# An explicit order of 1786 pieces in place of a list schedule, in a fused attention and gated MLP kernel

## The chip, the cores and the metric

The kernel runs on one core of one Trainium2 chip. The metric is the device time of one execution in microseconds (us), as a median of several runs. The core has five engines with a queue of instructions each: TensorE (PE, matrix products; PEld is its weight load), VectorE (DVE), ScalarE (ACT), GpSimd (POOL) and SyncE (SP), which here only issues DMAs. Each engine takes its own instructions strictly in the order in which the program lists them, and waits on semaphores for what other engines and DMAs have to deliver first.

## The reference

```python
def _attn_ref(q, k, v, n_sink, window):          # B, H, S, D = 4, 8, 768, 64
    scores = scale * np.matmul(q, k.transpose(0, 1, 3, 2))
    keep = is_sink | in_window                    # 4 sink keys, and the last 128 keys
    scores = np.where(keep, scores, -1000000000.0)
    a = np.exp(scores - np.max(scores, axis=-1, keepdims=True))
    a = a / (np.sum(a, axis=-1, keepdims=True) + 1e-09)
    return np.matmul(a, v)

def _moe_ref(x, w_in, w_spatial, b_spatial, w_out):   # x: 4, 768, 512
    h = np.maximum(x @ w_in, 0.0)                     # 512 -> 1024
    u, v = h[..., :512], h[..., 512:]
    v_n = (v - mu) / np.sqrt(var + 1e-06)             # over the last axis
    v_s = np.einsum('ts,bsd->btd', w_spatial, v_n) + b_spatial[None, :, None]
    return (u * v_s) @ w_out
```

The attention's output, its heads put side by side, is the x of the second function.

## The kernel before

There are 4 batches b, each of 6 tiles t of 128 positions. A tile is worked in two halves of four heads; the half number i = 2 * (6 b + t) + half runs from 0 to 47. Nearly all products run in f16, with each f32 operand split into a high and a low half (`high`, `low`, `low_scaled`, L577 to L612), so that one product is three passes: high by high, high by low, low by high (`three`, L619).

The work is cut into 1786 pieces, each one closure for one engine, registered by `plan.add` with a name, the engines that may take it, a price, and what it reads and writes. The pieces by name:

- Weights: `w_in 0` (the half of w_in that makes u), `w_in 1` (the half that makes v) and `w_out` come as f64 words; each of 12 chunks is loaded (L616), decoded (ACT L641, DVE L643 and L646, POOL L649) and split (`... split`: high L583 to L592, low L607 on DVE or the pair L609 and L610 on POOL). `w_sp` is f32, six chunks of 128x768, loaded and split likewise.
- Attention, for each half i: `score` (PE L844, eight products into four PSUM banks "sc"), four `mask` (DVE L849), four `exp` (ACT L854), `p high` and `p low` (a 128x1024 copy and a subtraction), two DMA transposes `turn high` and `turn low` issued by SP (L921), then `av` (PE L963 to L971). After both halves of a tile: `divide` (DVE L977 to L979) and a turn of x into xT, by PE transposes in the first tiles (`x cross`, L1013 and L1029) and by DMA later (`x turn`, L1000). Tiles 0 and 1 of batch 0 do their attention in f32 with PE transposes (`p cross`, L884).
- MLP: `ps_v` (PE, L622 and L1055) and `v relu`, `v stats`, `v root`, `v norm`, `vn high`, `vn low` for each tile; `ps_u` and `u relu` for each pair of tiles c0 and quarter d; `ps_s` (PE, all six vn tiles of a batch by w_sp), `gate`, `times`, `g high`, `g low` for each (b, c0, d); `ps_o` (PE L1164), `o copy` (L1175, L1177) and `o store` for each output tile. `ps_v`, `ps_u`, `ps_s`, `ps_o` and the PE transposes share two PSUM banks.
- Range checks (`v check`, `w check`, `check`, L704 to L763): v of batch 0 and the weights are read again, and one flag is formed: three DVE steps, a PE transpose (L751), three more DVE steps (L754 to L756). Every engine loads the flag at the end (L1229), and a general path follows if it is set.

`Plan.order` (L281) is a list scheduler: it plays the pieces through with their prices, with ring sizes and with ranks from the table `WHEN`, takes at each step the piece that can start first on an engine that may take it, and so fixes the engine of each piece and the order of each engine's queue. Where its model leaves PE idle ahead of a piece, `warm` (L519) puts fill products ahead of it, 128x248 products on the identity (L526) that nobody reads; the trace shows 56 of them. `check_ranges()` is called last, at L1214, and the planner leaves the transposing of the flag to the end of PE's queue. The order is emitted piece by piece under a manual schedule (L1215 to L1218).

Of the kernel before, what the change touches and what calls it, by code (L numbers as in the profile page):

```python
# [58 lines left out]
def general_path(tc, wf, qk, v, w_in, w_sp, b_sp, w_out, out):  # L59

    nc = tc.nc
    with (
# [46 lines left out]
        for b in range(B):  # L109
# [112 lines left out]
WHEN = {  # L222
    "p cross": (-7645.87,), "x cross": (-946.982,), "x copy": (-7684.67,), "pt copy": (-1378.19,),
    "qk load": (-4637.88, 832.975), "k sink": (-5707.62, -5463.63), "k copy": (-1001.25, -1158.33),
    "score": (-8509.54, -5574.54), "mask": (-5653, -3159.62), "exp": (-3128.31, 26.9811),
    "p high": (-5712.46, -4860.97), "turn high": (1126.36, -4889.17), "sink high": (-4766.44, -660.912),
    "sink low": (-1161.58, -1729.28), "p low": (-4294.7, -1248.23), "turn low": (-7503.49, -1155.83),
    "av": (-7132.32, -4355.89), "divide": (-4638.21, -4891.2), "x high": (-4655.36, -1108.11),
    "x low": (-9179.28, 688.315), "x turn": (1169.15, -1217.83), "v load": (-5315.45, 1085.95),
    "v sum": (-6868.55, -1941.04), "v check": (807.025,), "w check": (-1093.24,), "check": (-1155.04,),  # L230
    "v sink": (-7755.39, -946.192), "v high": (-4580.5, -1033.28), "v low": (-5057.21, -4564.35),
    "ps_v": (-5726.43, -1424.26), "v relu": (-4061.2, -1875.91), "v stats": (-1602.66, -987.246),
    "v root": (-9057.1, -4615.84), "v norm": (-8861.23, 1176.72), "vn high": (-4790.37, -1623.78),
    "vn low": (1788.02, -4613.58), "ps_u": (698.347, -1389.6), "u relu": (-3425.42, -1209.25),
    "ps_s": (-1766.1, -3895.91), "gate": (-7760.54, -4767.95), "times": (-1391.34, -1703.34),
    "g high": (703.784, 1087.49), "g low": (-4790.01, 220.472), "ps_o": (-5395.94, -5449.72),
    "o copy": (-2357.65, 704.671), "o store": (-4810.26, -7722.48), "w_in 1 load": (1768.73, -2689.71),
    "w_in 1": (-5162.73, -533.079), "w_in 1 split": (-1242.8, -4597.23), "w_in 0 load": (-8938.98, 1073.29),
    "w_in 0": (-999.782, -5625.87), "w_in 0 split": (1151.13, -883.018), "w_sp load": (-905.754, -1162.84),
    "w_sp split": (-879.562, -1410.66), "w_out load": (-1070.21, -6959.45), "w_out": (-2070.07, -1261.38),  # L240
    "w_out split": (745.032, -1267.5), "q 0": (-7481.31,), "w 0": (-5528.28,), "w 1": (-4758.02,), "v 0": (-5236.43,),
    "w 2": (-1040.43,), "v 1": (-1241.46,), "w 3": (-873.723,), "v 2": (-8862.13,), "q 1": (-7703.79,),
}
GAP = {"o": 1.0228e-13, "pace": 0.09559, "pace 0": 0.65293, "s": 1.9808e-08, "u": 2.0431e-06, "w_in 0": 0.00052094, "w_in 1": 1.469e-13, "w_out": 12.175, "w_sp": 62.955}
CROSSED = 2
TURNED = 6
PACED = ("qk load", "k copy", "score", "mask", "exp", "p high", "p cross", "pt copy", "turn high", "sink high", "sink low",
         "p low", "turn low", "av", "divide", "x copy", "x high", "x low", "x turn", "x cross", "v load", "v sum", "v sink", "v high", "v low", "ps_v", "v relu",
         "v stats", "v root", "v norm", "vn high", "vn low")
IN_TURN = ("u", "vn", "q", "pexp", "pT", "p16", "xT", "x16", "av", "sc", "vraw")  # L250
STRICT = ("p16",)
LATENCY = {"PE": 0.25, "d": 0.15, "a": 0.18, "p": 0.12}
# [11 lines left out]
QUEUED = 3.0  # L264
TURNS_AHEAD = 3.66
WARM_FROM, WARM_SHARE, WARM_ONE = 4.0, 0.5, 0.108


class Plan:

    def __init__(self, rings, ring_of, warm):
        self.pieces, self.rings, self.ring_of, self.warm = [], rings, ring_of, warm

    def add(self, name, step, b, engines, time, f, reads=(), writes=(), dma=None, shared=False):

        if name in PACED:
            step = 2 * NT * b + (step - 2 * NT * b) * GAP["pace" if b else "pace 0"]
        rank = step + WHEN[name][min(b, len(WHEN[name]) - 1)]
        self.pieces.append((rank, len(self.pieces), engines, time, f, tuple(reads), tuple(writes), dma, shared))

    def order(self):  # L281
        ps = sorted(self.pieces, key=lambda x: x[:2])
        n = len(ps)
        place = {x[1]: i for i, x in enumerate(ps)}
        before, seen, users, takes = [set() for _ in ps], {}, {}, {}
        for _, k, _, _, _, reads, writes, _, _ in self.pieces:
            i = place[k]
            for key, wr in [(k, False) for k in reads] + [(k, True) for k in writes]:
                base, part = key[:2], key[2:]
                if not wr and base not in seen:  # L290
                    raise RuntimeError(f"plan: {key} is read before it is written")
                for j, part2, wr2 in seen.setdefault(base, []):
                    if (wr or wr2) and (part == part2 or not part or not part2):
                        before[i].add(j)
                seen[base].append((i, part, wr))
                users.setdefault(base, set()).add(i)
        after = [[] for _ in ps]
        for i, b in enumerate(before):
            b.discard(i)
            for j in b:  # L300
                after[j].append(i)
        turn = {}
        for i in range(n):
            for key in ps[i][5] + ps[i][6]:
                base = key[:2]
                ring = self.ring_of.get(base[0])
                if ring and base not in takes:
                    takes[base] = ring
                    turn.setdefault(ring, []).append(base)
        held = {r: [] for r in self.rings}  # L310
        slots = {r: [None] * n for r, n in self.rings.items()}
        left = {b: len(u) for b, u in users.items()}
        until = {b: 0.0 for b in users}
        taken = set()
        missing = [len(b) for b in before]
        ready = [0.0] * n
        free = {"PE": 0.0, "d": 0.0, "a": 0.0, "p": 0.0, "SP": 0.0, "port": 0.0}
        moved = 3.07
        idle, pe = {}, WARM_FROM
        open_ = [i for i in range(n) if not missing[i]]  # L320
        out, room_at = [], {}

        def room(i):

            t, new = 0.0, {}
            for base in dict.fromkeys(key[:2] for key in ps[i][5] + ps[i][6]):
                ring = takes.get(base)
                if ring is None or base in taken:
                    continue
                k = len(held[ring]) + new.get(ring, 0)  # L330
# [3 lines left out]
                if ring in STRICT:  # L334
                    old = slots[ring][k % len(slots[ring])]
                    if old and left[old]:
                        return None
# [938 lines left out]
```

## Time and profile before

| what | value |
| --- | --- |
| median of 3 runs | 434.6 us (433.96 to 435.53) |
| the profiled execution's own time | 430.26 us |
| its span, first to last instruction | 428.5 us |
| mean granted TensorE clock | 0.978 |
| busy PE, DVE, ACT, POOL | 400.3, 336.9, 228.2, 172.0 us |

Busy time of PE is from the first to the last moment at which a product is on its way, so a stretch can show PE busy though products follow one another at half their possible pace; how far PE got is read from its pieces, at the time that each takes when nothing holds it up. A granted clock of 1.00 is the 2.4 GHz level of TensorE; 0.50 would be the 1.2 GHz level, and values between are a mix of both within a stretch.

### The profile page before, as it was taken

The numbers are of one execution on the slowest core, as the hardware profiler recorded it, in microseconds if no ns is written. First come the engines' busy times: TensorE is split into PE (matmuls) and PEld (weight loads), VectorE is DVE, ScalarE is ACT, GpSimd is POOL, SyncE is SP. The second block draws the span as 40 slices with busy tenths as digits, with TensorE's granted clock in tenths as the row PEclk, the third lists the DMA queues.
The fourth block names the chain that finished last, engine by engine and source line by source line (L and its number), as shares of the span: only waits on it lengthen the run. The fifth ranks groups of instructions, "written<-read, shape, count | busy, mean of one in ns | idle before, by whom it ended". The sixth has DMA issues, their size and how long they took to land.

```text
span 428.5 us, 9641 instructions
## 1 busy us (share of the span) xinstructions
PE 400.3 (93%) x3561; PEld 283.3 (66%) x3561; DVE 336.9 (79%) x943; ACT 228.2 (53%) x527; POOL 172.0 (40%) x207
## 2 busy tenths in 40 slices
PE   5598987989999999999999999999999899999992
PEld 4376555657777856756876658576786586586771
DVE  3999999799999999888986973489899884553441
ACT  2799595679777876577774541266532211211100
POOL 4757967675878943656421220052133220100000
PEclk9699998989999999999999999999999999999997
DMA  6999898799999898999997802496998761001011
GB/s 222 306 337 236 231 204 172 180 189 229 230 247 193 179 221 150 253 218 194 205 229 209 121 29 59 86 140 119 142 204 243 243 148 50 24 26 50 0 50 57
DMA packets 139655, 70.98 MB, mean 166 GB/s; under 512 B 112464, under 2 KB 125776, under 8 KB 139600
## 3 DMA queue, kind: packets, MB, share of 16 engines
q1 hardware_dynamic: 139456, 70.28, 73.3%
q8 instruction: 30, 0.49, 0.5%
q14 instruction: 25, 0.20, 0.1%
q10 hardware_dynamic: 144, 0.00, 0.0%
HBM read 36.71 MB, written 6.29 MB: 100 GB/s over the span
## 4 chain that ended last, share of the span: by engine, by line
PE 63%; DVE 23%; DMA 5%; issue 4%; ACT 2%; POOL 1%; SPq 0%; DVEq 0%; ACTq 0%; POOLq 0%
PE ps_s L622 17%; PE ps_o L1164 14%; PE ps_v L622 11%; PE ps_u L622 10%; PE sc L844 6%; DVE pexp L849 5%; DVE p L599 4%; DVE vring L607 2%; DMA dec<-w_in 2%; DVE g L1149 2%; PE av L969 2%; DVE w L646 2%; DVE w L643 1%; PE av L971 1%; PE av L970 1%
## 5 line engine op out<-in xcount | busy, mean ns | idle before, releaser
L622 PE MATMUL ps_s<-wsp,vn 128*128 128x256 f16 x864 | 100.1, 273 | 1.3 <-ACT ob L1175 1.3
L854 ACT ACTIVATE pexp<-pexp,nm 128x260 f32<-128x260 f32 (+1 forms) x192 | 83.8, 484 | 25.8 <-DVE nm L849 25.2
L622 PEld LDWEIGHTS <-vn 128*128 128x128 f16 x864 | 83.4, 98 | 14.4 <-issue 3.1
L622 PE MATMUL ps_u<-xT,win 128*128 128x256 f16 x576 | 69.8, 275 | 3.2 <-DVE xT L1019 2.7
L599 POOL TENSOR_TENSOR p<-pexp,p 128x16 f16<-128x16 f32 (+2 forms) x47 | 47.5, 1015 | 44.1 <-ACT p L583 30.9
L1164 PE MATMUL ps_o<-wout,g 128*128 128x512 f16 x288 | 64.8, 379 | 0.3 <-ACT u L1115 0.3
L622 PEld LDWEIGHTS <-win 128*128 128x128 f16 x576 | 55.5, 99 | 14.3 <-issue 6.1
L844 PE MATMUL sc<-kring,q 64*128 64x260 f32 (+1 forms) x384 | 58.4, 405 | 6.3 <-DMA q<-qk_t 4.1
L622 PE MATMUL ps_v<-win,xT 128*128 128x512 f16 x264 | 62.1, 387 | 0.0
L844 PEld LDWEIGHTS sc<-kring,q 64*128 64x128 f32 x384 | 36.9, 195 | 22.2 <-DVE nm L849 6.8
L1081 POOL TENSOR_TENSOR rs<-rs,mhalf 128x1 f32<-128x1 f32 x24 | 17.4, 726 | 80.8 <-DVE rs L1078 80.0
L1137 DVE SCALAR_TENSOR_TENSOR g<-ps_s,b_bc 128x256 f32<-128x256 f32 x48 | 20.2, 420 | 37.6 <-PE ps_s L622 37.2
L1164 PEld LDWEIGHTS <-g 128*128 128x128 f16 x288 | 27.5, 98 | 32.8 <-issue 2.2
L622 PEld LDWEIGHTS <-xT 128*128 128x128 f16 x264 | 25.7, 99 | 29.1 <-issue 3.4
L1115 ACT ACTIVATE u<-ps_u 128x256 f32<-128x256 f32 x48 | 18.1, 377 | 45.8 <-PE ps_u L622 45.6
L969 PE MATMUL av<-vring,pT 128*128 128x65 f16 x328 | 34.0, 193 | 2.0 <-DVE x L979 2.0
L599 DVE TENSOR_TENSOR p<-pexp,p 128x1024 f16<-128x1024 f32 (+2 forms) x29 | 35.0, 1209 | 0.6 <-ACT p L583 0.6
L1175 ACT ACTIVATE ob<-ps_o 128x512 f32<-128x512 f32 (+1 forms) x24 | 13.9, 579 | 39.3 <-PE ps_o L1164 35.0
L971 PE MATMUL av<-vring,pT 128*128 128x65 f16 x328 | 33.9, 193 | 0.0
L970 PE MATMUL av<-vring,pT 128*128 128x65 f16 x328 | 33.9, 193 | 0.0
L969 PEld LDWEIGHTS <-pT 128*128 128x128 f16 x328 | 30.2, 97 | 4.4 <-issue 3.0
L970 PEld LDWEIGHTS <-pT 128*128 128x128 f16 x328 | 30.1, 97 | 0.7
(131 smaller groups left out, 661.8 us busy)
## 6 DMA issues: line engine op xcount, KB each, us to landing
vraw<-v_s SPq DMA_DIRECT2D x30, 260.0 KB, 4.1
out<-ob SPq DMA_DIRECT2D x24, 256.0 KB, 2.1
kring<-qk_t SPq DMA_DIRECT2D x23, 256.0 KB, 4.4
q<-qk_t SPq DMA_DIRECT2D x23, 256.0 KB, 3.9
dec<-w_in SPq DMA_DIRECT2D x8, 512.0 KB, 7.2
pexp<-w_in SPq DMA_DIRECT2D x8, 512.0 KB, 4.8
wsp<-w_sp_t SPq DMA_DIRECT2D x6, 384.0 KB, 4.8
dec<-w_out SPq DMA_DIRECT2D x4, 512.0 KB, 4.3
```

The lines of the kernel that those rows point to most:

```text
L599: eng[e].tensor_tensor(out=o, in0=x, in1=hi, op=ALU.subtract)
L622: nc.tensor.matmul(o, a, m, start=(i == 0), stop=(i == n - 1))
L844: nc.tensor.matmul(view(h + q)[0], tl("q", (b, t))[rows, hp, :], keys, start=True, stop=True)
L849: nc.vector.tensor_tensor_reduce(out=po, in0=o, in1=mask, scale=-0.125, scalar=3.0e38, op0=ALU.add, op1=ALU.min, accum_out=nm()[:, q:q + 1])
L854: nc.scalar.activation(po, po, AF.Exp, bias=nm()[:, q:q + 1], scale=-1.0)
L969: nc.tensor.matmul(o[:, h], ph, vh, start=(t < 2 and j == 0), stop=False)
L970: nc.tensor.matmul(o[:, h], ph, vl, start=False, stop=False)
L971: nc.tensor.matmul(o[:, h], pl, vh, start=False, stop=(j == nb - 1 and (t < 2 or h == HH - 1)))
L1081: nc.gpsimd.tensor_tensor(out=vals["rs", i], in0=vals["rs", i], in1=mhalf, op=ALU.pow)
L1115: plan.add("u relu", r, b, "a", 0.365, lambda e: nc.scalar.activation(tl("u", (b, c0))[:, d, :], tl("ps_u", i)[:, :TC], AF.Relu, scale=G_U ...
L1137: nc.vector.scalar_tensor_tensor(out=g(), in0=tl("ps_s", i)[:, :TC], scalar=G_S, in1=b_bc[:, t0:t0 + TC], op0=ALU.mult, op1=ALU.add)
L1164: nc.tensor.matmul(o, lead, wout[:, w, d, :], start=(d == 0 and j == 0), stop=(d == KC - 1 and j == 2))
```

## The change

The tables `WHEN`, `GAP`, `PACED` and others, the costs for the planner and the list scheduler go. In their place stands `ORDER`, 1786 words, one for each piece, in the order in which they are emitted. A word is the number of the piece (in the order of the `plan.add` calls), a letter for its engine (P is PE, S is SP, a ACT, d DVE, p POOL) and, for PE, the number of fill products ahead of it.

```diff
+ORDER = """
+107S 117S 108a 109a 116S 122P7 123d 129d 118S 35S 127d 120p 213p 262p 36a 37d 38d 121p 159p 125d 126a 110d 39p
+28S 29a 119S 134P2 137d 135d 139d 30d 138a 130a 128a 136a 140a 49S 51d 124a 131P11 158S 157S 50a 31d 32p 52d 141d
...
+1630a 1745P 1746d 1747d 1748a 1749d 1756P 1757d 1758d 1759d 1760d 1702P 1703d 1750P 1751a 1753P 1754a 1755S 1761P
+1762d 1726S 1752S 1763d 1764d 1765d 1766P 1767d 1768d 1769d 1770d 1771P 1772d 1773d 1774p 1775d 1776P 1781P 1777P
+1779d 1782P 1778a 1780S 1784d 1783a 1785S
+"""
...
     def order(self):
+        listed, left = [], set(range(len(self.pieces)))
+        for word in ORDER.split():
+            n = next(j for j, x in enumerate(word) if not x.isdigit())
+            i, e, fill = int(word[:n]), word[n], int(word[n + 1:] or 0)
+            engines, f, writes = self.pieces[i]
+            e = {"P": "PE", "S": "SP"}.get(e, e)
+            assert e == engines or e in engines
+            left.remove(i)
+            listed.append((self.warm(writes[0], fill, f) if fill else f, e))
+        assert not left
+        return listed
...
-        def low_scaled(name, step, b, n, views, scale, reads, writes, engines="dp"):
+        def low_scaled(name, step, b, n, views, scale, reads, writes):
 
             def f(e):
                 o, x, hi = views()
-                if e == "d":
-                    nc.vector.scalar_tensor_tensor(out=o, in0=x, scalar=scale, in1=hi, op0=ALU.mult, op1=ALU.subtract)
-                else:
-                    nc.gpsimd.tensor_scalar(x, x, scale, 1.0, op0=ALU.mult, op1=ALU.mult)
-                    nc.gpsimd.tensor_tensor(out=o, in0=x, in1=hi, op=ALU.subtract)
+                nc.vector.scalar_tensor_tensor(out=o, in0=x, scalar=scale, in1=hi, op0=ALU.mult, op1=ALU.subtract)
...
-                             [("ps_o", i)], [("ob", i, j)])
+                             [("ps_o", i), ("flag", 0)], [("ob", i, j)])
...
+            if b == B - 1:
+                check_ranges()
             for c0 in range(S // TC):
...
-        check_ranges()
         order = plan.order()
```

No instruction of the computation is added. Read off the list, piece by piece, against the order that the trace of before shows, this is what differs:

- The engine of a piece. `p high`: 38 on ACT and 6 on DVE (before 20 and 24). `p low`: 18 on DVE, 26 on POOL (26 and 18). `vn low`: 9 on DVE, 15 on POOL (17 and 7). `times`: 24 and 24 (34 on DVE, 14 on POOL). `x high`: 9 on ACT, 8 on DVE, 6 on POOL (20, 2, 1). Low halves of w_in, w_sp and w_out: all on DVE (11 of them were pairs on POOL); their high halves on ACT and DVE alone.
- Fill products: 25 (7, 2 and 11 ahead of the first three PE pieces, then 3, 1 and 1), before 56 (48 ahead of the first score, then 7 and 1).
- The first loads on SP: a 97.5 KB tile of v_sink, then the first halves of q and k (128 KB each), then the second half of k, then w_in. Before: four 512 KB chunks of w_in, v, both v_sink tiles, then k and q.
- The place of the attention halves in PE's queue: the first score is first in both; half 18 stands behind 79 us of PE work (before 71), half 22 behind 124 us (96), half 30 behind 162 (137), half 40 behind 226 (183), half 46 behind 261 (254). Between a score of the halves 22 to 45 and its own `av` lie 15.4 us of other PE work on average, 10.8 at the least (before 29.3 and 13.8).
- The first `ps_s` stands behind 66.1 us of PE work, before behind 71.8.
- The PE transpose of the flag stands ahead of `ps_o` (3, 1, 0), and the three DVE steps that form the flag ahead of the gates of the last c0; the last DVE pieces are the two halves of `o copy`.

## Rows read from the trace of the kernel before

**Rows 1.** Busy time in four stretches: start:end, length, then as headed (x: instructions).
```profile
core 0: us, PE busy (x) PEld busy (x) DVE busy (x) ACT busy (x) POOL busy (x), PEclk, DMA share, GB/s
0.00:15.18 15.18, 6.53 (x48) 5.30 (x49) 7.72 (x15) 7.04 (x14) 8.26 (x27) 0.96 0.79 246
15.18:50.00 34.82, 31.61 (x234) 23.18 (x235) 34.62 (x98) 28.76 (x66) 25.74 (x28) 0.92 1.07 290
0.00:107.72 107.72, 89.45 (x760) 63.64 (x761) 96.09 (x260) 79.01 (x188) 71.71 (x92) 0.94 0.94 232
152.28:420.66 268.38, 266.72 (x2342) 186.11 (x2341) 195.90 (x565) 114.59 (x263) 63.00 (x73) 1.00 0.63 134
```
**Rows 2.** Chain that ended last, in time: start us, us, what.
```profile
155.03 1.08 PE sc L844 x8
168.76 3.93 PE ps_s L622 x36
183.03 2.59 PE ps_v L622 x12
200.68 1.31 PE ps_u L622 x12
```
**Rows 3.** Timeline of the start: start us, us, engine, line, operation, tiles [idle before <-releaser].
```profile
1.18 2.91 SPq L616 DMA_DIRECT2D dec<-w_in  x4
...
6.72 1.54 SPq L814 DMA_DIRECT2D kring<-qk_t  x2
...
9.17 1.58 SPq L816 DMA_DIRECT2D q<-qk_t  x2
...
15.18 1.23 PE L844 MATMUL sc<-kring,q 64*128 64x128 f32 x8 [4.08 <-DMA q<-qk_t]
```
**Rows 4.** DMA issues: tiles, queue, count, KB each, median us to landing.
```profile
pT<-p SPq DMA_TRANSPOSE x88, 3.6
...
kring<-qk_t SPq DMA_DIRECT2D x2, 128.0 KB, 5.5
q<-qk_t SPq DMA_DIRECT2D x2, 128.0 KB, 4.8
```
**Rows 5.** Groups, 0 to 107.72 us, DVE then POOL: count | busy us, mean ns.
```profile
L599 DVE TENSOR_TENSOR p<-pexp,p 128x1024 f16<-128x1024 f32 x6 | 10.2, 1700 | 0.0
L607 DVE SCALAR_TENSOR_TENSOR vring<-vraw,vring 128x512 f16<-128x512 f32 x9 | 9.6, 1071 | 0.0
L607 DVE SCALAR_TENSOR_TENSOR win<-w,win 128x512 f16<-128x512 f32 x6 | 8.0, 1379 | 0.0
L588 DVE CAST p<-pexp 128x1024 f16<-128x1024 f32 x6 | 5.0, 832 | 0.1
L607 DVE SCALAR_TENSOR_TENSOR wsp<-wsp 128x768 f16<-128x768 f32 x1 | 1.8, 1751 | 0.0
...
L610 POOL TENSOR_TENSOR wsp<-wsp 128x768 f16<-128x768 f32 x5 | 9.5, 1894 | 0.4
L609 POOL TENSOR_SCALAR wsp<-wsp 128x768 f32<-128x768 f32 x5 | 5.9, 1174 | 0.1
```
**Rows 6.** One line's instructions on DVE, whole span: count, ns least/median/most.
```profile
L607 DVE SCALAR_TENSOR_TENSOR vring<-vraw,vring x23: 680/695/2120, 13.6 to 286.1; 128x512 f16<-128x512 f32 x23
```
**Rows 7.** Timeline, halves 4 and 27: score on PE, both transposes on SP.
```profile
26.68 1.15 PE L844 MATMUL sc<-kring,q 64*128 64x260 f32 x8
...
32.67 4.37 SPq L921 DMA_TRANSPOSE pT<-p  x2
...
159.57 1.15 PE L844 MATMUL sc<-kring,q 64*128 64x260 f32 x8
...
173.15 2.66 SPq L921 DMA_TRANSPOSE pT<-p  x2
```
**Rows 8.** Timeline of DVE at the end.
```profile
421.16 0.42 DVE L1177 TENSOR_SCALAR ob<-ps_o 128x256 f32<-128x256 f32 x1 [0.22 <-ACT ob L1175]
...
421.98 0.14 DVE L756 CAST flagi<-checks 1x1 int32<-1x1 f32 x1
```

More of the change, by code (lines that the diff above doesn't have):

```diff
@@ L220 @@
          "xT": 2, "g": 2, "g2": 6, "w32": 8, "xT32": 1}
[L222 to L243, printed above, removed]
@@ L269, with __init__ @@
+1762d 1726S 1752S 1763d 1764d 1765d 1766P 1767d 1768d 1769d 1770d 1771P 1772d 1773d 1774p 1775d 1776P 1781P 1777P
+1779d 1782P 1778a 1780S 1784d 1783a 1785S
+"""
 class Plan:
-    def __init__(self, rings, ring_of, warm):
-        self.pieces, self.rings, self.ring_of, self.warm = [], rings, ring_of, warm
+    def __init__(self, warm):
+        self.pieces, self.warm = [], warm
     def add(self, name, step, b, engines, time, f, reads=(), writes=(), dma=None, shared=False):
[L276 to L279, printed above, removed]
+        self.pieces.append((engines, f, tuple(writes)))
@@ L281, in order @@
     def order(self):
[L282 to L330, printed above, removed]
-                if ring in IN_TURN and turn[ring][k] != base:
-                    return None
-                j = new[ring] = new.get(ring, 0) + 1
[L334 to L337, printed above, removed]
-                    t = max(t, until[old] if old else 0.0)
-                    continue
-                ends = sorted(until[b] if b else 0.0 for b in slots[ring] if b is None or not left[b])
-                if len(ends) < j:
-                    return None
-                t = max(t, ends[j - 1])
-            return t
@@ L408, in order @@
-        if len(out) != n:
-            raise RuntimeError("plan: pieces left")
-        self.end = max(until.values())
-        final = []
-        for k, (t, i, f, e) in enumerate(out):
-            if i in idle:
-                _, since, key = idle[i]
-                count = int((t - max(since, room_at.get(i, 0.0))) * WARM_SHARE / WARM_ONE)
-                if count > 0 and self.takes_bank(key):
-                    f = self.warm(key, count, f)
-            final.append((t, k, f, e))
-        return [(f, e) for _, _, f, e in sorted(final, key=lambda x: x[:2])]
@@ L556, in fast_path @@
         }
-        rings = dict(RINGS, ksink=1, **BANKS)
-        rings.update({f"{kind}{j}": 1 for kind in ("kslot", "vslot", "vsink") for j in range(4)})
-        plan = Plan(rings, dict({k: r for k, (r, _) in makers.items()}, **{r: r for r in rings}), warm)
+        plan = Plan(warm)
         tiles = {}
@@ L624, in early @@
         def early(x, name, step, b):
-            return (x, 0) if b == 0 and x in WHEN else (name, step)
+            return (name, step)
         vals = {}
@@ L662, in w_in_half @@
                            lambda c=c, i=i, hi=hi: (win[:, 1, c, f0:f0 + 512], tl("w32", i), hi()), SW_IN,
-                           [("w32", i), ("win", half, (0, c))], [("win", half, (1, c))], "d" if half else "dp")
+                           [("w32", i), ("win", half, (0, c))], [("win", half, (1, c))])
         def w_spatial():
-            gap = GAP["w_sp"]
+            gap = 1
             for c in range(NT):
@@ L680, in w_out_all @@
         def w_out_all():
-            gap = GAP["w_out"]
+            gap = 1
             for c in range(KC):
@@ L859, in scores @@
                 queries, keys = [("q", (0, 0), hf)], [(f"kslot{kslot(0, 0)}", (0, 0), (0, hf))]
-            plan.add("score", i, b, "PE", 1.05 if t else 0.75, product, queries + keys, banks)
+            plan.add("score", i, b, "PE", 1.08 if t else 0.75, product, queries + keys, banks)
             for q in range(n):
```

186 lines of the change are left out of this document (93 added, 93 removed).

## The prediction

> **What bounds the kernel now.** Begin with busy time by stretch [rows 1]. From 152 us to 420.66 PE is busy 266.7 of 268.4 us at a clock of 1.00: there TensorE is the bound, and only less waiting on it can help. In the first 107.72 us, up to the first `ps_s`, DVE is busy 96.1 us, and it has nothing to do before 7.86: of 99.9 us it works 96.1. There VectorE is the bound. PE looks busy for 89.4 of these 107.7 us, but that is elapsed pipeline time. What PE has got through is counted in pieces at their unhindered time [rows 2]: 1.08 us for a score, 3.93 / 2 = 1.97 for a `ps_s`, 2.59 for a `ps_v`, 1.31 for a `ps_u`. Ahead of the first `ps_s` stand 19 scores (18.8 us, the two halves without earlier keys being shorter), 12 `ps_u` (15.7), 6 `ps_v` (17.4, the two in f32 taken at 3.5), 15 `av` (13.5) and 12 crosses (6.3): 71.8 us of PE work, done in 107.72. So PE loses 107.7 - 71.8 = 35.9 us ahead of that piece.
>
> The rest is accounted in the same way. All PE pieces sum to 378 us; PE's last product ends at 420.66 [rows 1], and 428.5 - 420.66 = 7.8 us of tail follow. Lost later is then 428.5 - 378 - 35.9 - 7.8 = 6.8 us. The forecast replaces three of these terms: 35.9, 6.8 and 7.8. The 378 stays, as the change adds and removes no product but fill products.
>
> The start is in the timeline [rows 3]: SP issues w_in from 1.18, k only at 6.72 and q at 9.17, and the first score waits for q until 15.18. So 15.2 of the 35.9 us are the wait for q, and 20.7 are lost behind DVE.
>
> **The change: the order of the start.** Ahead of q and k now stands one v_sink tile. At some 0.75 us an issue (1.54 and 1.58 us for two [rows 3]) q and the first k half are issued between about 2.0 and 3.5 us. They land 4.8 and 5.5 us after issue at the median [rows 4], so the first score starts between 6.6 and 8.9 us; I take 7.9, 7.3 earlier than now. What pays is w_in: it moves behind four issues on SP, 3 us, and its decoding starts that much later. DVE has the sink's split and the first masks to fill this with.
>
> **The order of DVE's work, and low halves on DVE.** I counted the pieces that stand ahead of the first `ps_s` on DVE in both orders. At mean durations the old order has 88.5 us there. Removed: 5 `p high` at 0.83, 3 `p low` at 1.70, 5 masks at 0.35, 4 sink splits at 0.5, and some 5.3 us of smaller ones, 18.3 us in all. Added: 5 low halves of w_sp at 1.75, 2 of w_in at 1.38, 4 high halves of w_in at about 0.5, 2 decodes at 0.7 and four pieces of 0.2 to 0.8, 17.1 us [rows 5]. So DVE's own list is level, about 87.3 us: the change moves as much onto DVE as it takes off it. ACT has 73 us ahead of that point before and 65 after, so it is not late.
>
> What changes is POOL. It loses five w_sp pairs at 1.17 + 1.89 us (15.4 us), two w_in pairs (3.8) and six high halves (6.0), and gains two `p low` at about 2.1 and an x high: 68 us become 44. This matters to DVE because its durations stretch when POOL works: the same 128x512 subtraction takes 0.68 us at the least, 2.12 at the most [rows 6], and 1.07 on average in the first 107.7 us; the win form of the same size averages 1.38 [rows 5]. That excess is 9 x 0.39 = 3.5 us for v and 6 x 0.69 = 4.1 us for win; with the decodes, the `p low` and the rest of DVE's forms against their own least I make it 17 us in the stretch. A third of POOL's work goes, so I take a third of the excess off DVE, 6 us; the ends are 0, if what stays on POOL meets DVE as often, and 14, if the w_sp pairs did most of the harm. 87.3 - 6 = 81.3 us. By the Trainium skill, "SBUF — State Buffer", section "SBUF: two separate sides", GpSimd and a VectorE instruction with two SBUF inputs take turns on one shared port pair, each holding it for its whole instruction; the spread of 0.68 to 2.12 us fits that. By it the added two-input pieces on DVE would be exposed too, and the gain would be 4 to 5 us instead of 6.
>
> DVE's idle time while it is the bound: 3.8 us now; I take 4, and 7 if the later w_in leaves a hole (the share of the DMA engines is 1.07 between 15 and 50 us [rows 1], but DVE idles only 0.2 us there, so DMA is not what it waits for).
>
> DVE is then through with what the first `ps_s` needs at 7.9 + 81.3 + 4 = 93.2 us. That piece now stands behind 66.1 us of PE work (three scores, two `av` and one `ps_u` fewer), so PE loses 93.2 - 66.1 = 27.1 us ahead of it, where it lost 35.9. Ends: 6.6 + 73.3 + 4 - 66.1 = 17.8; and 8.9 + 87.3 + 1.5 + 7 - 66.1 = 38.6, where the 1.5 is for w_sp pieces that POOL stretches on DVE.
>
> **The order of the attention.** Halves 22 to 45 now have 15.4 us of PE work between a score and its `av`, 10.8 at the least, where 29.3 stood before. In between lie masks, exps, the two copies and two turns. For half 4, which was wanted early, the second turn was issued 9.2 us after the score's end (27.83 to 37.04); for half 27, 15.1 us (160.72 to 175.81) [rows 7]; a landing comes 3.6 us after its issue [rows 4], some 2.2 after the end of a pair of issues. So the chain takes 11.3 us when hurried and about 17.5 unhurried. PE executes its queue in order: behind an `av` that waits, everything waits. I take it that queues with little in them give the hurried time, and leave the later loss at 6 us; ends 3 and 13. Fewer `p high` on DVE and later deadlines for v and w checks speak for that.
>
> **The flag.** The last copy on DVE ends at 421.58, and the flag's last step at 422.12 [rows 8]. With the flag formed earlier the end hangs on the copies: -0.5 us, tail 7.3 (ends 7.0 and 7.8). The PE transpose of the flag, 0.2 us, now stands ahead of three groups of `ps_o`; PE would wait there if the re-read weights were not summed by then, but ACT is busy only 115 of the last 268 us [rows 1] and has room. The three DVE steps now delay the last gates by some 0.5 us, which the `ps_o` queued on PE covers; without that cover they cost that 0.5.
>
> **The sum.** 378 + 27.1 + 6 + 7.3 = 418.4 us of span, against 428.5. The profiled execution took 430.26, 1.8 above its span, and stands 4.3 under the median of the runs, so 418.4 + 1.8 + 4.3 = 424.5. Low: 378 + 17.8 + 3 + 7.3 = 406.1, or 412.2. High, with the first loss at its worst: 378 + 38.6 + 6 + 7.8 = 430.4, or 436.5.
>
> **Rivals.** *Nothing gained: DVE stays the bound, undisturbed by POOL's relief.* With no excess removed and 7 us of idle behind the later w_in, 7.9 + 87.3 + 7 - 66.1 = 36.1 lost, and 378 + 36.1 + 6.9 + 7.5 = 428.5: 434.6, the old time. For it: DVE's list is level and q is not what DVE waits for. Against: the earlier first score, and the row's spread of 0.68 to 2.12.
>
> *Slower: the attention chain no longer fits.* If the chain from score to `av` keeps its 17.5 us where the list leaves 15.4, PE waits in proportion over the 131 us of work between scores 22 and 45: 131 x (17.5 / 15.4 - 1) = 17.9 us, 442.4. It outweighs the gain of 10.1 from 15.4 x (1 + 10.1 / 131) = 16.6 us on. For it: half 27. Against: half 4 [rows 7], and that DVE's and ACT's queues drain faster in that stretch.
>
> *The clock.* Before the first score stand 48 fill products, of 6.5 us, and the granted clock is 0.96 up to 15.18 and 0.92 up to 50 [rows 1]. With 7 there and PE waiting on DVE between its pieces, PE could stay at the 1.2 GHz level until about 50 us; it has some 24 us of work by then, which would take twice as long, and the first 42 us would not hold them: about 7 us, 431.5. Against: the clock stayed at 0.92 with half of PE's time lost. The Trainium skill, "TensorE: Matmul & The Clock Gate", section "What's actually happening", has the throttled level as the default that activity releases; no row here shows PE at that level for long.
>
> *It doesn't do what it says.* Hardly possible: an order is executed as listed. What could differ is only a wait that a new order adds.
>
> **How the numbers follow.** Forecast 0.68; nothing gained 0.12; chain 0.11; clock 0.09. A measurement tells 0.3%, 1.3 us, from no change. Faster: the forecast's 0.68, the clock's 0.09 and 0.03 of "nothing gained"; same: 0.06 of it; slower: its last 0.03 and the chain's 0.11. The range, 412 to 437, takes in the ends of the first loss, the clock and nothing gained; left out are the chain (0.11) and some 0.08 of the forecast beyond its ends.
>
> **What would show it.** In the new profile: a first score at 7 to 9 us; the first `ps_s` near 93; POOL busy less by a third up to there, and the 128x512 low halves on DVE nearer to 0.9 than to 1.07 and 1.38; no wait of PE above 2 us on a turn after 120 us; the last copy, not the flag, as DVE's last step. Wrong if the first `ps_s` starts after 103, if waits of `av` for DMA sum to more than 6 us, or if the granted clock up to 50 us is near 0.5.

## The result, and the profile after

The changed kernel takes 411.98 us (411.48 to 412.96, four runs) against 435.06 us for the kernel before: 0.947 of it, with an interval of 0.944 to 0.950. The profiled execution took 412.96 us, its span is 411.2. That is 23 us faster where 10 were forecast, and just below the range of 412 to 437.

First the stretches, by the columns of [rows 1]: to where PE's loss stops growing (58.73), to the first `ps_s` (85.09), and from there to 403.50.

```profile
0.00:58.73 58.73, 49.04 (x398) 34.10 (x399) 49.46 (x167) 46.39 (x101) 31.88 (x56) 0.97 0.95 252
0.00:85.09 85.09, 75.31 (x657) 52.78 (x658) 73.36 (x237) 68.83 (x150) 44.78 (x70) 0.98 0.99 251
85.09:403.50 318.41, 314.40 (x2872) 222.68 (x2870) 231.56 (x695) 161.83 (x371) 116.42 (x141) 1.00 0.72 154
```

The first `ps_s` starts at 85.09 with 66.1 us of PE work ahead of it: 19.0 us are lost up to there, 36 before. POOL is busy 44.8 us up to there, 71.7 before. PE's pieces show where the loss arises: 6.2 us at the first score, 12.2 at the first `p cross`, 18.2 at 58.7 us, and then almost nothing until 320. From 59 us on PE is the bound, 49 us earlier than before. The granted clock rose too, from 0.94 to 0.98 ahead of the first `ps_s`, but in the kernel before DVE idled only 3.8 us there, so PE's clock cannot have cost more than that.

The same groups as [rows 5], in the first 85.09 us (columns as there):

```profile
L522 DVE SCALAR_TENSOR_TENSOR wsp<-wsp 128x768 f16<-128x768 f32 x6 | 6.3, 1050 | 0.0
...
L522 DVE SCALAR_TENSOR_TENSOR vring<-vraw,vring 128x512 f16<-128x512 f32 x8 | 6.0, 766 | 0.0
...
L522 DVE SCALAR_TENSOR_TENSOR win<-w,win 128x512 f16<-128x512 f32 x8 | 5.4, 683 | 0.0
...
L554 DVE TENSOR_SCALAR w<-dec 128x512 int32<-128x512 int32 x9 | 4.0, 459 | 0.1
```

The low half of w_in takes 0.683 us where it took 1.379, and that of v 0.766 where it took 1.071; the least in [rows 6] is 0.680. That of w_sp takes 1.050 where the only one on DVE before took 1.751.

The start, in the timeline of all engines (columns as [rows 3]):

```profile
1.17 0.42 SPq L527 DMA_DIRECT2D vsraw<-v_sink  x1
1.64 0.41 SPq L727 DMA_DIRECT2D q<-qk_t  x1
2.10 0.95 SPq L725 DMA_DIRECT2D kring<-qk_t  x2
...
4.96 0.33 SPq L727 DMA_DIRECT2D q<-qk_t  x1
...
6.22 1.23 PE L755 MATMUL sc<-kring,q 64*128 64x128 f32 x8
...
10.64 0.72 PE L755 MATMUL sc<-kring,q 64*128 64x128 f32 x8 [2.60 <-DMA q<-qk_t]
...
13.46 1.11 PE L795 MATMUL pt<-ident,pexp 128*128 128x128 f32 x4
```

The second score waits for the second half of q, issued at 4.96 behind two loads of w_in. PE's longest waits by releaser, over the whole span (total, times, longest):

```profile
PE sc L444 <- POOL m_second L387: 4.6, 1, 4.6
PE sc L755 <- DMA q<-qk_t: 2.6, 1, 2.6
PE ps_v L533 <- DVE g L1048: 1.8, 1, 1.8
...
PE av L874 <- DMA pT<-p: 0.7, 1, 0.7
```

An `av` waits for a turn once, for 0.7 us: the attention chain is no bound. And the end, PE's last products and then DVE's last row:

```profile
399.02 5.34 PE L1075 MATMUL ps_o<-wout,g 128*128 128x512 f16 x24
```

```profile
404.40 0.42 DVE L1088 TENSOR_SCALAR ob<-ps_o 128x256 f32<-128x256 f32 x1 [0.17 <-PE ps_o L1075]
```

The last product ends at 404.36, and 411.2 - 404.36 = 6.8 us of tail follow; the copy is DVE's last step, not the flag [rows 8].

### The profile page after: what moved, and what is told of

Read it like the earlier page. It is cut to its first block, busy times and chain, and to the rows that moved or that the text cites. A ratio compares the mean times of both kernels' runs of the same rounds, so it can differ in the third digit from the quotient of the medians.

```text
span 411.2 us, 9563 instructions
## 1 busy us (share of the span) xinstructions
PE 390.6 (95%) x3530; PEld 275.7 (67%) x3530; DVE 305.8 (74%) x933; ACT 231.4 (56%) x522; POOL 161.2 (39%) x211
## 4 chain that ended last, share of the span: by engine, by line
PE 81%; DMA 9%; DVE 6%; ACT 1%; issue 1%; SPq 0%; ACTq 0%
PE ps_s L533 21%; PE ps_u L533 13%; PE ps_o L1075 13%; PE ps_v L533 11%; PE sc L755 10%; DMA pexp<-w_in 4%; PE av L880 2%; PE av L881 2%; PE av L882 2%; PE ps_v L966 2%; DMA q<-qk_t 1%; DMA vraw<-v_s 1%; DMA xT<-x 1%; PE av L874 1%; DVE pexp L760 1%; DMA words<-window 1%
## 5 line engine op out<-in xcount | busy, mean ns | idle before, releaser
L765 ACT ACTIVATE pexp<-pexp,nm 128x260 f32<-128x260 f32 (+1 forms) x192 | 84.7, 485 | 31.1 <-DVE nm L760 30.4
L515 POOL TENSOR_TENSOR p<-pexp,p 128x1024 f16<-128x1024 f32 (+2 forms) x48 | 56.7, 1189 | 57.8 <-ACT p L499 39.1
L533 PE MATMUL ps_u<-xT,win 128*128 128x256 f16 x576 | 68.8, 273 | 0.8 <-ACT vr L979 0.8
L533 PE MATMUL ps_v<-win,xT 128*128 128x512 f16 x264 | 60.4, 379 | 2.6 <-DVE g L1048 1.8
L755 PE MATMUL sc<-kring,q 64*128 64x260 f32 (+1 forms) x384 | 53.5, 392 | 3.0 <-DMA q<-qk_t 2.6
L755 PEld LDWEIGHTS sc<-kring,q 64*128 64x128 f32 x384 | 33.3, 189 | 17.9 <-issue 7.9
L499 ACT CAST p<-pexp 128x1024 f16<-128x1024 f32 (+2 forms) x70 | 43.1, 633 | 1.5 <-ACT pexp L765 0.5
L1086 ACT ACTIVATE ob<-ps_o 128x512 f32<-128x512 f32 (+1 forms) x24 | 13.8, 577 | 42.1 <-PE ps_o L1075 28.8
L1052 POOL TENSOR_TENSOR g<-g,u 128x256 f32<-128x256 f32 x24 | 18.0, 752 | 49.2 <-DVE g L1048 45.7
L992 POOL TENSOR_TENSOR rs<-rs,mhalf 128x1 f32<-128x1 f32 x24 | 14.6, 610 | 44.1 <-DVE rs L989 44.1
L880 PEld LDWEIGHTS <-pT 128*128 128x128 f16 x328 | 30.2, 97 | 2.2 <-issue 1.3
```

The lines of the kernel that those rows point to most:

```text
L499: nc.scalar.copy(o, x)
L515: eng[e].tensor_tensor(out=o, in0=x, in1=hi, op=ALU.subtract)
L533: nc.tensor.matmul(o, a, m, start=(i == 0), stop=(i == n - 1))
L755: nc.tensor.matmul(view(h + q)[0], tl("q", (b, t))[rows, hp, :], keys, start=True, stop=True)
L765: nc.scalar.activation(po, po, AF.Exp, bias=nm()[:, q:q + 1], scale=-1.0)
L880: nc.tensor.matmul(o[:, h], ph, vh, start=(t < 2 and j == 0), stop=False)
```

## The experiments

Every kernel is an order of the same 1786 pieces. "Old" kernels have the order that the planner had made, written out as a list (instruction for instruction the kernel before); "new" ones have the changed list. Where low halves go back to POOL, they are the pairs of before. "Lost" is counted as in the prediction, PE's start of a piece less the PE work ahead of it: at the first `ps_s`, and at the first `ps_s` of the last batch. It is read from one profiled execution of each kernel; the changed list run twice gave 19.0 and 19.2, 26.3 and 24.2.

| kernel | us, median | ratio to before, interval | lost at first `ps_s` | at the last batch's |
| --- | --- | --- | --- | --- |
| before | 433.0 to 435.06, five medians | | 36.0 | 43.2 |
| the change | 411.98 | 0.947 (0.944 to 0.950) | 19.0 | 26.3 |
| old_again | 432.56 | 0.998 (0.995 to 1.001) | 35.4 | 45.1 |
| old_low_dve | 428.84 | 0.987 (0.983 to 0.991) | 33.1 | 42.2 |
| old_qk_first | 434.62 | 1.003 (0.999 to 1.006) | 37.1 | 45.6 |
| new_low_pool | 429.65 | 0.989 (0.985 to 0.993) | 28.7 | 43.7 |
| new_pool_reads | 424.88 | 0.979 (0.975 to 0.984) | 33.5 | 38.5 |
| new_pool_writes | 419.02 | 0.966 (0.962 to 0.970) | 26.2 | 32.0 |
| new_p_old | 433.81 | 0.999 (0.995 to 1.003) | 29.0 | 46.3 |
| new_loads_old | 420.28 | 0.970 (0.964 to 0.975) | 27.9 | 33.0 |
| old_new_engines | 445.92 | 1.031 (1.024 to 1.038) | 38.1 | 59.9 |
| new_old_engines | 465.15 | 1.072 (1.067 to 1.078) | 38.7 | 78.7 |
| new_again | 411.19 | 0.949 (0.944 to 0.953) | 19.2 | 24.2 |
| new_q_early | 411.41 | 0.949 (0.946 to 0.953) | 19.2 | 23.0 |
| new_wout_pool | 419.03 | 0.967 (0.963 to 0.972) | 18.6 | 31.9 |
| new_phigh_old | 421.22 | 0.971 (0.967 to 0.975) | 27.0 | 34.9 |
| new_no_fill | 412.07 | 0.950 (0.945 to 0.954) | 21.5 | 26.0 |
| new_flag_last | 412.55, one execution | | 19.0 | 25.7 |

### How the old kernel scatters, and its low halves alone

The list of before instead of the new one, unchanged (old_again), and with the engine letter of eleven words changed (old_low_dve):

```diff
-107S 117S 108a 109a 116S 122P7 ...
+1700d 28S 35S 42S 49S 29a ...
...
-48p 55p 64p 66p 68p 72p 74p 81p 89p 97p 105p
+48d 55d 64d 66d 68d 72d 74d 81d 89d 97d 105d
```

> The kernel before, its order written out as a list: the same instructions. It is run for the scatter of its executions. If the 4 to 5 us between the profiled execution (430.3) and the median (434.6) are one lucky execution, the timed spans here lie near 432 to 434 and the profiled one with them; if the clock makes it, the spans and the granted clocks go together, with a lower clock in the longer ones.

> The old order, with nothing changed but that the 11 low halves of weights that were pairs on POOL run on DVE, each in its old place. Theory A (POOL's reads stretch DVE's instructions): DVE takes on 6.6 us ahead of the first ps_s (5 x 1.05 + 2 x 0.69), POOL loses 19 us there, and of the 17 us by which DVE's forms ran above their least some 11 go; win low falls from 1.38 to about 0.7 us, v low from 1.07 to about 0.8; net 4 to 5 us off: 429 to 431. Theory B (the order decides, durations do not depend on POOL): DVE gets 6.6 to 10 us longer while it is the bound, 440 to 445.

The old order's ten executions lie between 430.45 and 433.97, with granted clocks of 0.977 to 0.989 that are only loosely lower in the longer ones (433.97 at 0.977, 433.17 at 0.988, 430.45 at 0.987). So the profiled execution of before, 430.26, lies at the fast end; the clock as the cause of the scatter is neither shown nor excluded. With the low halves on DVE 4 us come off. Theory A holds in sign and size:

```profile
L525 DVE SCALAR_TENSOR_TENSOR vring<-vraw,vring 128x512 f16<-128x512 f32 x9 | 10.0, 1109 | 0.0
...
L525 DVE SCALAR_TENSOR_TENSOR wsp<-wsp 128x768 f16<-128x768 f32 x6 | 6.5, 1081 | 0.0
L525 DVE SCALAR_TENSOR_TENSOR win<-w,win 128x512 f16<-128x512 f32 x8 | 6.4, 825 | 0.0
```

```profile
L525 DVE SCALAR_TENSOR_TENSOR wsp<-wsp x6: 945/948/1750, 45.6 to 92.6; 128x768 f16<-128x768 f32 x6
```

(Groups of DVE up to 107 us; then w_sp by itself, ns least/median/most.) win and w_sp fall from 1.38 and 1.75 to 0.83 and 1.08 us. The five w_sp halves that came over take 0.94 to 0.95; the one that DVE had before still takes 1.75, beside a `vn low` of POOL. v stays at 1.1: three of its nine take 1.4 to 2.6 us, with a decode's sum or a `p low` of POOL beside each. Ahead of the first `ps_s` DVE takes on seven pieces, and the 148 that it had there take 84.8 us in place of 91.5. POOL is busy 20 us less up to there, so DVE got back 0.34 us for each of them.

### The first loads

```diff
 old_qk_first: q and k of the first tile ahead of all, 7 fill products ahead of the first score
+117S 116S 118S 119S 1700d 28S 35S ... 122P7 ...
 new_loads_old: the 13 first loads of the old list ahead of the new list
+28S 35S 42S 49S 210S 107S 111S 157S 116S 117S 158S 118S 119S 108a 109a 122P7 ...
```

> The old order, but the first tile of q and k is loaded ahead of everything, and 7 in place of 48 fill products stand ahead of the first score. Theory A (DVE is the bound of the start, q only one of its inputs): the first score moves from 15.2 to about 6 to 8 us, but DVE's chain hardly moves, the first ps_s starts within 3 us of 107.7, total 431 to 435. Theory B (the wait for q is lost time that adds): 7 to 9 us come off, 426 to 428.

> The new order with SP's first 13 loads in the old order (w_in first, q and k as the last of them). The first score moves from 6.2 to about 15 us. If the start carries part of the gain, as the prediction had it (7.3 us), the loss ahead of the first ps_s grows from 19 to 24 to 28 and the total to 417 to 421; if w_in's earlier decodes make up for it, as in the old order, where early q and k gave nothing, 412 to 414.

In the old order the early q brings nothing. The timeline of PE says why:

```profile
6.13 1.23 PE L761 MATMUL sc<-kring,q 64*128 64x128 f32 x8
18.22 1.43 PE L761 MATMUL sc<-kring,q 64*128 64x128 f32 x8 [10.87 <-DVE nm L766]
```

The first score starts 9 us earlier and the second one 1 us later: it waits 10.9 us for the first one's masks, which stand on DVE behind decodes and splits of w_in. In the new order, whose DVE list begins with masks, the old loads cost 8.3 us, nearly the whole shift of the first score (15.2 for 6.2) and of the first `ps_s` (94.0 for 85.1). The start is worth about what the prediction put on it, 7.3, but only together with DVE's order.

### What POOL's reads do to DVE

```diff
+        idle = const.tile([P, S], F32, name="idle")
+        nc.gpsimd.memset(idle, 0.0)
...
-            for f, e in order:
+            for n, (f, e) in enumerate(order):
                 f(e)
+                if n in (30, 66, 92, 133, 166, 205, 241, 297, 331, 375, 418, 452):
+                    nc.gpsimd.tensor_tensor(out=idle, in0=idle, in1=idle, op=ALU.add)   # new_pool_reads
+                    nc.gpsimd.memset(idle, 0.0); nc.gpsimd.memset(idle, 0.0)            # new_pool_writes
```

The memset that fills `idle` is in both kernels; each of the last two lines is in one of them. new_pool_reads also has `add` for `max` in two reductions, which the cut leaves out: one in the general path and one among the last steps of the range checks, behind the stretch read here.

> The new kernel with 12 sums of a 128x768 f32 tile with itself put on POOL, spread over the DVE pieces ahead of the first ps_s; nobody reads them, DVE's own list is unchanged. They give POOL back about 24 us of work with SBUF reads. Theory A (POOL's reads stretch DVE): v low rises from 0.77 and win low from 0.68 to above 1.0 us, DVE's time ahead of the first ps_s grows by 5 to 9 us, lost there 24 to 28 instead of 19.0, total 417 to 421. Theory B (what counts is who waits for POOL's queue): DVE's forms keep their durations, and this run and new_pool_writes cost the same, 1 to 4 us.

> As new_pool_reads, but each sum is replaced by two memsets of that tile: POOL is busy for about as long and writes, but reads nothing. Theory A: DVE's forms stay near their least (v low below 0.85, win low below 0.75), and only what waits for POOL is later: 412 to 415. Theory B: the same time as new_pool_reads. If the writes stretch DVE too, it is POOL's busy time and not its reads.

DVE's groups up to 85 us, first with the sums, then with the memsets:

```profile
L526 DVE SCALAR_TENSOR_TENSOR vring<-vraw,vring 128x512 f16<-128x512 f32 x7 | 9.1, 1305 | 0.0
L526 DVE SCALAR_TENSOR_TENSOR win<-w,win 128x512 f16<-128x512 f32 x8 | 7.7, 966 | 0.0
L561 DVE SCALAR_TENSOR_TENSOR w<-dec,w 128x512 int32<-128x512 int32 x8 | 6.6, 829 | 0.1
L558 DVE TENSOR_SCALAR w<-dec 128x512 int32<-128x512 int32 x8 | 6.2, 785 | 0.0
```

```profile
L526 DVE SCALAR_TENSOR_TENSOR vring<-vraw,vring 128x512 f16<-128x512 f32 x7 | 6.0, 873 | 0.0
...
L558 DVE TENSOR_SCALAR w<-dec 128x512 int32<-128x512 int32 x8 | 5.4, 690 | 0.0
L561 DVE SCALAR_TENSOR_TENSOR w<-dec,w 128x512 int32<-128x512 int32 x8 | 5.4, 685 | 0.1
L526 DVE SCALAR_TENSOR_TENSOR win<-w,win 128x512 f16<-128x512 f32 x8 | 5.4, 682 | 0.0
...
L999 DVE TENSOR_SCALAR vr<-vr,mv,rs 128x512 f32<-128x512 f32 x4 | 3.0, 761 | 0.4 <-POOL rs L996 0.4
...
L510 DVE TENSOR_SCALAR win<-w 128x512 f16<-128x512 f32 x4 | 2.3, 578 | 0.0
L519 DVE TENSOR_TENSOR p<-pexp,p 128x16 f16<-128x16 f32 x1 | 2.0, 2024 | 0.0
```

The 141 DVE pieces that the first `ps_s` needs take 73.5 us in the changed kernel, 88.8 with the sums and 79.9 with the memsets. The 12 sums are 18.7 us (1.56 each), not the 24 expected; they cost DVE 15.3 us, 0.8 for each microsecond of POOL. The 24 memsets, 17.7 us (0.74 each), cost it 6.4. So theory A holds, at two to three times the expected size, and theory B falls. The granted clock up to the first `ps_s` is 0.91 in both, so it does not tell them apart. The total of new_pool_writes came out above what theory A expected (419.0 for 412 to 415), and below new_pool_reads. The memsets do stretch forms with a single input: the decode (0.459 to 0.690), the `v norm` (0.540 to 0.761) and the high half of w_in (0.420 to 0.578), some 3.9 of the 6.4 us. The rest is not theirs: a subtraction of 16 columns (0.163 to 2.024) and one of v (0.69 to 1.43) meet a `p low` and an `x high` of POOL, which read. The two of v that overlap a memset alone take 0.68 and 0.69, and w_in's and the decode's with two inputs stay at 0.68. The memset of the tile itself puts the first score 0.6 us later.

### The old engines in the new order, and the new ones in the old

```diff
 new_low_pool: the eleven low halves as pairs on POOL
-48d 55d 64d 66d 68d 72d 74d 81d 89d 97d 105d
+48p 55p 64p 66p 68p 72p 74p 81p 89p 97p 105p
 new_wout_pool: only 81p 89p 97p 105p
 new_p_old: p high and p low of every half, 52 words
-225a 241a 347a 380a ... 294p 335p 384p ... 527d 541d
+225d 241d 347d 380d ... 294d 335d 384d ... 527p 541p
 new_phigh_old: only p high, 26 words
 new_old_engines, old_new_engines: all engine letters of the other list
```

> The new order, but the 11 low halves that the old list gave to POOL are pairs on POOL again, in their place in the new list. Theory A: DVE loses 6.6 us of its own work ahead of the first ps_s and its other forms stretch again by 8 to 11 us (win and v low back above 1.0 us), and what waits for the pairs, 3 us each, waits longer: 414 to 418. Theory B: the order alone carries the gain, 411 to 412.

> The new order with only the four low halves of w_out as pairs on POOL; those of w_in and w_sp stay on DVE. With all eleven on POOL the time was 17.7 us longer, 9.7 of them lost ahead of the first ps_s (at 85 us), the rest between 120 and 137. If the two stretches are two independent costs: 7 to 8.5 us longer than the new kernel, 418 to 421, with the first ps_s at 85 again. If the second loss came from the first (pieces late by 10 us meeting the pairs): 412 to 415.

> The new order with p high and p low of every half on the engine that the old list gave them (52 pieces change). Ahead of the first ps_s DVE takes on 6 p high (5.0 us at 0.83) and two p low net (2.6 us), POOL loses two of 2.1 us. Theory A: DVE is the bound up to about 58 us, where four of the six p high and two or three of the p low stand; 3 to 6 us more lost, 415 to 418. Theory B (the low halves alone carry the gain): 412 to 413.5.

> The new order with only p high on its old engines: 22 go from ACT to DVE and 4 back, 18 x 0.83 = 15 us more on DVE in all, which is busy 306 of 411 us. If DVE's free time takes them in: up to 5 us longer, 412 to 417. If DVE's queue is in effect the bound until 300 us, since it is taken in order: 8 to 16 us longer, 420 to 428, and PE's loss grows through the whole run and not only ahead of the first ps_s. The rest of the 21.8 us of p high and p low together is p low's.

> The old order with every piece on the engine that the new list gives it (198 pieces change engine, none its place). Theory E (the share of work between DVE, ACT and POOL carries the gain, the order little): DVE's work falls from 337 to about 306 us, its forms run near their least, the first score stays at 15: 416 to 421. Theory O (order and engines only work together, since each piece was put where its engine was free): 426 to 435.

> The new order with every piece on the engine that the old list gave it. Theory E: the gain goes, and the old engines in places not meant for them cost more: 434 to 450 (the low halves alone cost 17.7 us, p high and p low alone 21.8). Theory O: the order itself (early q and k, first ps_s behind less PE work) keeps 5 us or more of the gain: 420 to 430.

These are the large effects, and most of what I expected of them was too small. The low halves back on POOL cost 17.7 us. new_wout_pool shows two independent places: without the w_in and w_sp pairs the first `ps_s` is at 85 again, and 7 us remain. Its timelines show how, on POOL, ACT and PE in turn:

```profile
112.76 0.62 POOL L527 TENSOR_SCALAR w<-w 128x512 f32<-128x512 f32 x1
113.46 1.15 POOL L528 TENSOR_TENSOR wout<-w,wout 128x512 f16<-128x512 f32 x1
114.58 1.27 POOL L566 TENSOR_TENSOR w<-w,wtmp 128x512 int32<-128x512 int32 x1
```

```profile
115.88 0.63 ACT L503 ACTIVATE wout<-w 128x512 f16<-128x512 f32 x1 [4.93 <-POOL w L566]
119.26 0.42 ACT L684 ACTIVATE g<-g 128x256 f16<-128x256 f32 x1 [2.75 <-POOL g L1058]
...
120.92 0.59 ACT L985 ACTIVATE vr<-ps_v 128x512 f32<-128x512 f32 x1
```

```profile
121.55 2.72 PE L539 MATMUL ps_u<-xT,win 128*128 128x256 f16 x12 [5.56 <-ACT vr L985]
124.20 2.11 PE L761 MATMUL sc<-kring,q 64*128 64x260 f32 x8
```

The last sum of a decode stands on POOL behind two pairs; ACT waits 4.9 us for it to split that chunk, and then 2.8 us for a `times` that stands on POOL behind a third pair; behind this on ACT stands the `v relu` that frees a PSUM bank; PE waits 5.6 us for the bank. After the wait the granted clock is 0.70 from 121.5 to 130 us, and the `ps_u` and the score there take 2.72 and 2.11 us, about twice as long as elsewhere, which costs 2 us more. Each engine took its queue in order, and the list put the pieces so closely that a delay passed through three of them.

`p high` and `p low` back on their old engines take the whole gain, 21.8 us, 9.2 of it by `p high` alone; by difference, if the two add up, 12.6 by `p low`. They put more work on DVE. Stretches of 100 us from 100 to 300, the changed kernel, new_p_old and new_phigh_old (columns as above):

```profile
100.00:200.00 100.00, 100.00 (x946) 68.63 (x944) 82.20 (x251) 65.94 (x159) 45.57 (x57) 1.00 0.93 193
200.00:300.00 100.00, 100.00 (x1003) 71.00 (x1001) 80.29 (x256) 64.79 (x144) 39.94 (x47) 1.00 0.88 175
```

```profile
100.00:200.00 100.00, 96.07 (x886) 66.27 (x885) 87.52 (x246) 64.31 (x160) 38.67 (x47) 1.00 0.86 183
200.00:300.00 100.00, 96.67 (x970) 67.83 (x967) 88.25 (x253) 56.63 (x136) 41.51 (x50) 1.00 0.86 171
```

```profile
100.00:200.00 100.00, 98.22 (x940) 68.51 (x937) 86.64 (x248) 64.47 (x161) 47.43 (x55) 1.00 0.92 188
200.00:300.00 100.00, 100.00 (x1018) 70.55 (x1017) 87.88 (x268) 59.36 (x140) 41.34 (x49) 1.00 0.92 179
```

With DVE at 80 to 82% PE has no gap for 200 us. In new_p_old, with DVE at 88%, PE loses 3 to 4 us in each hundred, and the loss grows from 29 to 46 us; its longest waits over the whole run, the start aside, are for DVE: 5.4 us in all for masks, 6.1 for `g`. But DVE's share alone does not decide it: new_phigh_old has it at 87 and 88% too, and loses 1.8 us in the first hundred and none in the second. How much is DVE's amount of work, and how much the places of the pieces in its queue, is not shown.

The last two runs say what the gain is not. The new engines in the old order make that kernel 12 us slower, and in the first 100 us DVE is then busy only 80 of them while PE waits:

```profile
0.00:100.00 100.00, 83.02 (x660) 57.41 (x660) 79.83 (x237) 76.21 (x173) 46.32 (x70) 0.91 0.90 229
```

The new order on the old engines is 32 us slower than before. Theory E of the old order (416 to 421) falls, and theory O's 426 to 435 was too low as well: neither part holds the gain. The two exchanged lists were the worst of all; the 434 to 450 expected of new_old_engines had the direction and not the size.

### Small terms

new_again is the changed kernel once more, new_q_early moves one load, new_no_fill takes the fill products out, new_flag_last moves the flag's last two pieces to the end.

```diff
 new_q_early
-118S 35S 127d ... 28S 29a 119S
+118S 119S 35S 127d ... 28S 29a
 new_no_fill
-122P7 134P2 131P11 187P3 191P1 252P1
+122P 134P 131P 187P 191P 252P
 new_flag_last
-1702P 1703d 1750P ... 1780S 1784d 1783a 1785S
+1750P ... 1780S 1702P 1784d 1783a 1703d 1785S
```

> The changed kernel itself once more, beside the others of this call: 411.5 to 413.

> The new kernel with one load moved: the second half of the first q is issued ahead of the first two w_in chunks and not behind them. The second score waits 2.6 us for it, until 10.64; it should start near 7.5. If the wait is on the path of the start, 1 to 2.5 us come off: 409.5 to 411. If w_in's decode, 0.4 us later, or the exps hold the first p cross at 13.5 anyway: 412 to 413.

> The new kernel without its 25 fill products. Clock theory: the granted clock falls below 0.9 in the first 20 to 30 us and PE works longer there while it is the one to wait for: 413 to 417. If PE waits for DVE in that stretch anyway, or the first real products hold the clock up: 411 to 412.5.

> The new order with the PE transpose of the flag and the three DVE steps after it put back to where the old list had them, behind the last products and copies. By the prediction the tail from PE's last ps_o product to the end of the span grows by about 0.5 us, from 6.8 to 7.3 to 7.8. If the end hangs on the last stores and not on DVE's last step: no change, 6.8.

new_q_early: the second score moves from 10.7 to 8.2, the first `p cross` not (14.0 for 14.1 in new_again): no difference. new_no_fill: none either, though PE starts slower. The third score of the changed kernel, then the third score of new_no_fill and two stretches of it (columns as above):

```profile
14.51 1.32 PE L755 MATMUL sc<-kring,q 64*128 64x260 f32 x8
```

```profile
14.86 2.10 PE L757 MATMUL sc<-kring,q 64*128 64x260 f32 x8
```

```profile
0.00:20.00 20.00, 8.61 (x43) 6.07 (x44) 11.54 (x43) 10.12 (x23) 9.02 (x33) 1.00 0.83 295
40.00:50.00 10.00, 10.00 (x87) 5.98 (x85) 8.77 (x27) 8.27 (x19) 3.48 (x5) 0.84 0.68 135
```

Up to 19 us the products of new_no_fill take twice their time, as at the 1.2 GHz level, though the column PEclk says 1.00: the trace's first record of the clock in that run stands at 19.2, and for the time before it the durations decide. From 40 to 50 us, after waits of PE, the granted clock is 0.84. PE has lost 2.5 us more at the first `ps_s` (21.5), and at the last batch the difference is gone (26.0).

new_flag_last, PE's last products and DVE's last rows:

```profile
397.81 5.34 PE L1077 MATMUL ps_o<-wout,g 128*128 128x512 f16 x24
```

```profile
403.81 0.28 DVE L667 TENSOR_REDUCE checks<-ps_row 1x1 f32<-1x128 f32 x1 [0.19 <-PE ps_row L664]
...
404.29 0.14 DVE L669 CAST flagi<-checks 1x1 int32<-1x1 f32 x1
```

The tail is 410.8 - 403.15 = 7.6 us in place of 6.8 (6.9 in new_again): the flag's place is worth 0.8 us by these two executions, somewhat more than the 0.5 expected. The other lists with the early flag have tails of 6.3 to 6.9 us. In the total, which scatters by more, it can't be seen.

## Why the prediction was wrong

The direction and the place were right (VectorE as the bound of the start, the wait for q, POOL's share in DVE's durations). The size was wrong by 12.5 us, and the terms of the sum account for it:

- **PE lost ahead of the first `ps_s`**: 27.1 forecast, 19.0 measured, -8.1. It is the term of DVE's list, 81.3 forecast and 73.5 measured. Of the 88.5 us taken as the old list its pieces in the trace make 91.5 (+3.0); those that go took 21.4, not 18.3 (-3.1); those that come took 11.6, not 17.1 (-5.5); and the 122 pieces that stand in both lists fell from 70.1 to 61.9, 8.2 where I took 6 (-2.2). So the step that failed is "Added: 5 low halves of w_sp at 1.75, 2 of w_in at 1.38". These durations were themselves stretched by POOL's work beside them: the 1.38 for the most part by pairs and decodes, the 1.75, a single instance, by a `vn low`. I charged the stretch to the new list and took a third of all excess off again. At what they take in the changed kernel, 1.05 and 0.68, these seven come 4.9 us cheaper. The relief of what stays was mis-sized by less: 8.2 us for the 27 that POOL lost, 0.30 for each, as in old_low_dve (0.34), where "a third of the excess", 6 us for 24, was 0.25. The 0.8 of new_pool_reads is the price of sums set down one after another beside a busy DVE, and not what this change gave back. DVE's idle time came to 5.4 us, not 4. (POOL's own sum has a slip: 68 less the 25.2 listed plus some 5 is 48, not 44; measured are 71.7 and 44.8.)
- **The first score**: 7.9 forecast, 6.2 measured; the second waited for its q until 10.6. "Earlier first score" pays 8.3 us in this order (new_loads_old) and nothing in the old (old_qk_first).
- **Lost later**: 6 forecast; from 85.09 to 404.36 are 319.3 us for 311.9 of work, 7.4 lost. Within its ends.
- **Tail**: 7.3 forecast, 6.8 measured; the flag is worth 0.8.
- **From the span to the median**: I added 6.1 us, of which 4.3 was the distance of the profiled execution of before to the median. Measured are 0.8: 411.98 - 411.2. This is 5.3 us of the error. This is the second step that failed, "stands 4.3 under the median of the runs, so". The old order's executions lie between 430.3 and 436.9, and the profiled one is the fastest of them; the distance was a property of that execution, not of the kernel, and should have gone into the range.

-8.1 - 5.3 + 1.4 - 0.5 = -12.5, which is 411.98 - 424.5.

The rivals. *Nothing gained* fell with POOL's relief. *The attention chain*: score to second landing took 12.8 us on average in the halves 22 to 45 (9.7 to 16.9), and the tightest `av` had 1.0 us to spare; in the old order, which left 29.3 us for it, it took 24.6. The step "I take it that queues with little in them give the hurried time" was nearly right, 12.8 for 11.3. *The clock*: in the changed kernel the granted clock is 0.91 up to 20 us and 1.00 from 40 to 50; without any fill product PE does run at the lower level up to 19 us, as the rival has it, but the 7 us that it put on this do not come: 412.07. What the prediction had no case for is the interplay: it read each engine's list for its sum, and so a list on other engines would have come out nearly as good. new_low_pool, new_wout_pool and the two exchanged lists cost 7 to 53 us, and in new_wout_pool the traces show a delay that no sum of work has.

What stays open is what the two parts of the change, order and engines, are worth each: the exchanged lists only show that neither works with the other's old partner. In new_low_pool DVE's remaining pieces took 78.5 us for 67.3 ahead of the first `ps_s`, which is 5.0 more than all had taken in the changed kernel; the other 4.7 of the 9.7 us lost there are idle time of DVE.

## What to carry to other kernels

Price a moved instruction at what it will take beside its new neighbours: look for the least and the most of a row, ask which engine makes the difference, and where the change removes that cause, use the least for what stays as well as for what comes. A sum of work per engine bounds a stretch from below only; with queues taken in order, each of the two lists here was good only with its own engines, so change both together, or expect that the first one alone can lose. And a profile's distance to the median is one draw: put it into the range.

## What the runs showed of the hardware

In new_pool_reads a microsecond of POOL's sums, which read SBUF, cost DVE 0.8 us; moving POOL's pairs away gave back 0.30 to 0.34 for each. DVE's subtractions with two inputs stay at 0.68 us beside POOL's memsets and rise to 0.97 to 1.31 on average in the kernel with the sums; the decode with one input rises beside both (0.46 to 0.69 and 0.79). Two rows show that it matters which started first: in the changed kernel a low half of w_in that starts at 34.10, ahead of a `p low` on POOL at 34.27, takes 0.68 us; in old_low_dve a low half of v that starts at 73.43, inside a `p low` that ends at 75.43, takes 2.55. The Trainium skill, "SBUF — State Buffer", section "SBUF: two separate sides", says that a VectorE instruction with two SBUF inputs excludes only GpSimd instructions that read SBUF, and one in a two-port mode any GpSimd instruction; its section "Who interferes with whom" counts `tensor_scalar`, which the decode is, among those that can be in such a mode. The two runs agree with it; that the decode was in that mode is inferred from its 0.42 us for 512 elements, where two inputs take 0.69.
